# A transformer block on one core: fewer first dummy matmuls, in fp32; one filler matmul moved; the second scale sums made to wait for all their rows

## Chip, cores and metric

One core of one Trainium2 chip. The metric is the device time in microseconds; the 6 executions of the kernel before lie within 0.4% (243.81 to 244.73). A "span" is the time between the first and last instruction of the profiled execution, 1.2 to 1.5 us less than that execution's device time.

## The reference

A diffusion transformer block: six modulation vectors from `c`, layer norm with scale and shift, attention with two heads, a gated residual, a second layer norm, an MLP, a gated residual. All inputs are bf16.

```python
B, N, D = (2, 256, 1152)          # H = 2, Dh = 576, F = 4608
mod = (_silu(c) @ w_mod).reshape(B, 6, 1, D)
shift_a, scale_a, gate_a, shift_m, scale_m, gate_m = [mod[:, i] for i in range(6)]
h = _layernorm(x, axis=-1) * (1 + scale_a) + shift_a
qkv = (h @ wqkv).reshape(B, N, 3, H, Dh)
# ... attention, x = x + gate_a * a, second layer norm, MLP, gated residual (cut)
```

Only the first 20 us matter here: layer norm of x, `1 + scale_a` from `w_mod`, and the K projection.

## The kernel before

The kernel lists units of work per engine with the regions that they read and write. A scheduler derives the waits and emits each engine's instructions; TensorE keeps the written order. A semaphore is a counter on which engines wait. Every instruction other than a DMA adds 1 to its engine's semaphore (an "increment" below), and a DMA adds 16 to its own:

```python
for (k, v) in waits[ins.gidx]:
    eng_handle.wait_ge(dma_sems[k[1]] if k[0] == "d" else sems[k[1]], v)   # shortened
bi = ins.fn(eng_handle)
if ins.dma_sem is not None:
    bi.then_inc(dma_sems[ins.dma_sem], 16)
else:
    bi.then_inc(sems[e], 1)
```

The loads, in the order in which they are issued: x, the first scale weights (columns of 4 of 9 groups, in three parts of rows), K rows 0 to 3, the second scale weights (the other 5 groups, three parts), K rows 4 to 8, and so on.

```python
for (ka, kb) in ((0, KC), (KC, KT)):                      # KC = 4, KT = 9
    w = (kb - ka) * P
    for k0, k1 in ((0, 3), (3, 6), (6, 9)):
        dma(WSC[:, k0:k1, ka * P:kb * P], wmod_v[...], (k1 - k0) * P * w * 2, "ld_sc%d_%d" % (ka, k0), run=w * 2)   # shortened
    for kt in range(ka, kb):
        dma(WK[:, kt, :], wqkv_v[:, kt, D:2 * D], P * D * 2, "ld_wk%d" % kt, run=2304)
```

Dummy matmuls on zeros keep TensorE busy before there is work. The K projection runs in two parts: the first (K rows 0 to 3) while the second scale weights arrive, then 45 matmuls of 2 columns ("second scale sums"), then the second part. VectorE scales the K input between the sums and the second part; filler matmuls ("k12") in two pieces cover that.

```python
dve(270, lambda e: e.memset(Q4B, 0.0), [], [Q4B], "zq4b")
for i in range(5):
    S.unit("pe", 430.0, "warm_a%d" % i)
    mm(ps32(5), IDENT, Q4B, True, True)
CT_PS = ps16(6, 0, 18)
S.unit("pe", 100, "c_T")
tr(CT_PS, CSB[0:18, :], IDENT[0:18, 0:18])                # then tanh (ScalarE) and silu (VectorE)
# ... cut
def k12(part):
    kts = ((range(3), ()), (range(3, KC), range(KC)))[part]
    # ... 3 matmuls in the first piece, 5 in the second
for kt in range(KT):
    if kt == 6:
        k12(0)
    mod_kt(WSC, kt, 0, "scb_%d" % kt, (KC, KT))           # 5 matmuls of 2 columns
hk(KC, 0)                                                 # VectorE scales the K input
# ... cut
k12(1)
```

## Time and profile before

| | before |
|---|---|
| device time, median of 6 runs | 244.24 us (243.81 to 244.73) |
| span of the profiled execution (one of 243.62 us) | 242.3 us |
| TensorE busy | 98% of the span |
| first transposes / start of the K projection | 7.98 / 11.18 us |
| second scale sums / second K part | 17.44 / 19.63 us |

The profile is read in this order: the page's slices and its chain, the chain in order of time, then what the weight loads (PEld) waited for. The lines are in the prediction below. Starts of single matmuls, landings of DMAs and DMA packets come from the same trace's records, where each landing of x or of weights is 16 updates of a semaphore, read here as one from each of the 16 DMA engines.

### The profile page before, as it was taken

The page shows a single profiled execution, that of the slowest core. Times are in us where ns is not written, and L with a number is a line of the kernel's source. Part 1 is how long each engine was busy: PE and PEld are TensorE (multiplying, and loading weights), DVE is VectorE, ACT ScalarE, POOL GpSimd, SP SyncE. Part 2 cuts the span into 40 slices and gives each one's busy share as a digit, 9 for nine tenths or more (in the row PEclk, how much of TensorE's full clock was granted, in tenths as well). Part 3 has the DMA queues.
Part 4 walks back from the last instruction along what each step waited for, and adds up shares of the span by engine and source line. Part 5 has one row for each costly group of instructions (what it writes and reads, how often), then busy time and mean ns, then how long its engine had stood idle before and what let it go on. Part 6 is the DMA issues. An engine that isn't in the chain of part 4 may idle for free.

```text
span 242.3 us, 4076 instructions
## 1 busy us (share of the span) xinstructions
PE 238.4 (98%) x1763; PEld 147.5 (61%) x1763; DVE 120.3 (50%) x218; ACT 67.0 (28%) x136; POOL 21.2 (9%) x39
## 2 busy tenths in 40 slices
PE   7999999999999999999999999999999999999996
PEld 2698854556667666898444444444566656656676
DVE  3814388696997699789999500000022222111112
ACT  5820350355424107973233322222000000000000
POOL 1400000000021186400000000020000000000000
PEclk9999999999999999999999999999999999999999
DMA  6999999999996999989953498012000000000001
GB/s 241 330 381 392 391 392 391 397 413 405 391 356 196 351 395 391 391 266 394 314 164 82 150 320 313 0 29 72 0 16 19 16 16 19 16 16 16 19 24 27
DMA packets 30140, 51.59 MB, mean 213 GB/s; under 512 B 1703, under 2 KB 15787, under 8 KB 30123
## 3 DMA queue, kind: packets, MB, share of 16 engines
q1 hardware_dynamic: 29680, 50.14, 58.0%
q0 software_dynamic: 416, 1.19, 1.6%
q8 instruction: 14, 0.23, 0.4%
q14 instruction: 3, 0.02, 0.0%
q10 hardware_dynamic: 27, 0.00, 0.0%
HBM read 50.14 MB, written 1.19 MB: 212 GB/s over the span
## 4 chain that ended last, share of the span: by engine, by line
PE 97%; DVE 2%; POOL 0%; issue 0%; ACT 0%; DVEq 0%; POOLq 0%
PE psum L688 95%; PE psum L691 2%; DVE arena L739 1%; DVE arena L760 0%; POOL arena L711 0%; DVE arena L740 0%; DVE arena L1284 0%; DVE arena L1285 0%; POOL arena L710 0%; ACT arena L726 0%; DVE arena L727 0%; DVE arena L732 0%; DVE arena L742 0%; POOL arena L717 0%; POOL arena L715 0%
## 5 line engine op out<-in xcount | busy, mean ns | idle before, releaser
L688 PE MATMUL psum<-arena 128*128 128x384 bf16 (+10 forms) x1674 | 234.9, 306 | 1.6 <-POOL arena L711 1.5
L688 PEld LDWEIGHTS psum<-arena 128*128 128x128 bf16 (+3 forms) x1674 | 142.3, 97 | 90.0 <-issue 3.8
L1079 DVE SCALAR_TENSOR_TENSOR arena<-arena 128x1152 f32<-128x1152 bf16 x32 | 44.7, 1414 | 0.6
L1284 DVE TENSOR_TENSOR arena<-psum,arena 128x384 f32<-128x384 f32 (+3 forms) x14 | 7.0, 501 | 68.0 <-PE psum L688 68.0
L1193 ACT ACTIVATE arena<-psum 128x512 bf16<-128x512 f32 (+1 forms) x44 | 22.4, 520 | 42.7 <-PE psum L688 42.7
L683 ACT ACTIVATE arena<-psum 128x512 bf16<-128x512 f32 (+6 forms) x37 | 19.6, 549 | 39.5 <-PE psum L688 37.1
L685 DVE CAST arena<-psum 128x512 bf16<-128x512 f32 (+3 forms) x13 | 8.2, 641 | 11.4 <-PE psum L688 11.3
L669 POOL DMA_DIRECT2D dit_scratch<-arena x3 | 1.8, 616 | 115.7 <-DVE arena L685 58.9
L1161 POOL TENSOR_TENSOR arena<-arena 128x384 f32<-128x384 f32 x12 | 10.9, 910 | 10.8 <-DVE arena L1160 9.5
L1106 DVE CAST arena<-psum 72x32 bf16<-72x32 f32 x1 | 0.2, 186 | 21.3 <-PE psum L688 21.3
L739 DVE BATCH_NORM_STATS2 arena<-arena 128x6 f32<-128x384 f32 (+1 forms) x18 | 9.5, 552 | 0.1
L1166 ACT ACTIVATE arena<-arena 128x1152 bf16<-128x1152 f32 x4 | 5.3, 1345 | 11.9 <-DVE arena L1165 11.9
L691 PEld LDWEIGHTS psum<-arena 128*128 128x128 bf16 (+1 forms) x89 | 5.8, 98 | 2.5 <-issue 0.8
L1160 DVE TENSOR_TENSOR arena<-psum,arena 128x384 f32<-128x384 f32 x12 | 6.5, 549 | 1.6 <-DMA arena<-dit_scratch 1.6
L1285 DVE TENSOR_TENSOR arena<-arena 128x384 bf16<-128x384 f32 (+3 forms) x14 | 7.0, 501 | 0.5
L691 PE MATMUL psum<-arena 128*128 128x128 bf16 (+1 forms) x89 | 7.1, 219 | 0.1
L1180 DVE TENSOR_SCALAR arena<-psum,arena 128x128 bf16<-128x128 bf16 x20 | 5.4, 341 | 1.9 <-PE psum L691 1.9
L1183 ACT ACTIVATE arena<-psum,arena 128x128 bf16<-128x128 bf16 x16 | 6.0, 456 | 0.9 <-PE psum L688 0.6
L1086 DVE TENSOR_REDUCE arena<-arena 128x36 f32<-128x1152 f32 x4 | 5.4, 1348 | 0.0
L1083 DVE STREAM_TRANSPOSE arena<-arena 128x1152 f32<-128x1152 f32 x4 | 5.4, 1364 | 0.0
L1009 ACT ACTIVATE arena<-psum,arena 128x256 bf16<-128x256 f32 x8 | 3.7, 472 | 1.3 <-PE psum L688 0.9
L743 POOL TENSOR_TENSOR arena<-arena 128x1 f32<-128x1 f32 x6 | 3.6, 596 | 2.0 <-DVE arena L742 2.0
(48 smaller groups left out, 44.9 us busy)
## 6 DMA issues: line engine op xcount, KB each, us to landing
arena<-in_w_fc_dram SPq DMA_DIRECT2D x9, 1152.0 KB, 7.3
arena<-in_w_fc_dram SPq DMA_DIRECT2D x4, 2592.0 KB, 17.2
arena<-in_wqkv_dram SPq DMA_DIRECT2D x18, 288.0 KB, 10.2
arena<-in_w_mod_dram SPq DMA_DIRECT2D x3, 1728.0 KB, 20.2
arena<-in_w_mod_dram SPq DMA_DIRECT2D x3, 864.0 KB, 13.7
arena<-in_w_mod_dram SPq DMA_DIRECT2D x9, 288.0 KB, 10.5
arena<-in_wqkv_dram SPq DMA_DIRECT2D x1, 2592.0 KB, 16.6
arena<-in_wo_dram SPq DMA_DIRECT2D x1, 2592.0 KB, 24.4
```

What stands on the lines that cost most here:

```text
L683: act(c_act(n), lambda e: e.activation(out=dst, in_=src, func=ACTF.Copy), [src], [dst], name)
L685: dve(c_dve_psum16(n) if psum16 else c_dve_psum32(n), lambda e: e.tensor_copy(dst, src), [src], [dst], name)
L688: S.instr(lambda e: e.matmul(o, lhsT=l, rhs=r, start=st, stop=sp, **kw), reads=[l, r], writes=[o])
L691: S.instr(lambda e: e.transpose(o, i_, idn), reads=[i_, idn], writes=[o])
L739: dve(550, lambda e, s=s, o=o: e.bn_stats(out=o, in_=s), [s], [o], "bn_%s_%d" % (tag, ci))
L1079: dve(1270, lambda e, w=w, s=s, acc=acc: e.scalar_tensor_tensor(out=acc, in0=w, scalar=s, in1=acc, op0=ALU.mult, op1=ALU.add), [w, s, acc] ...
L1160: dve(550, lambda e, o=o, ga=ga, x1c=x1c: e.tensor_tensor(out=x1c, in0=o, in1=ga, op=ALU.mult), [o, ga], [x1c], "wo_t1_%d_%d" % (t, ci))
L1161: S.op("pool", 930, lambda e, xs=xs, x1c=x1c: e.tensor_tensor(out=x1c, in0=x1c, in1=xs, op=ALU.add), reads=[x1c, xs], writes=[x1c], name=" ...
L1183: act(440, lambda e, o=o, dst=dst, s1=s1, s2=s2: e.activation(out=dst, in_=o, func=ACTF.Identity, scale=s1, bias=s2), [o, s1, s2], [dst], ...
L1193: act(c_act(ntok), lambda e: e.activation(out=dst, in_=o, func=ACTF.Gelu_apprx_tanh), [o], [dst], "gelu_%d_%d" % (f, tok0))
L1284: dve(c_dve_psum32(w), lambda e, o=o, gm=gm, t1=t1: e.tensor_tensor(out=t1, in0=o, in1=gm, op=ALU.mult), [o, gm], [t1], "fc2_t1_%d_%d" % ( ...
L1285: dve(c_dve_32(w), lambda e, t1=t1, x1c=x1c, ost=ost: e.tensor_tensor(out=ost, in0=t1, in1=x1c, op=ALU.add), [t1, x1c], [ost], "fc2_out_%d ...
```

## The change

The intent, as far as the code tells: let the transpose of c come earlier (fewer, longer dummies in front of it, with one fp32 matmul in place of several in bf16), shorten the hole ahead of the second K part by moving a filler matmul, and let TensorE's sequencer wait once for all rows of the second scale weights.

```diff
-        dve(270, lambda e: e.memset(Q4B, 0.0), [], [Q4B], "zq4b")
-        for i in range(5):
-            S.unit("pe", 430.0, "warm_a%d" % i)
-            mm(ps32(5), IDENT, Q4B, True, True)
+        ZF = sb(O_Q4B, 2048, F32)
+        dve(400, lambda e: e.memset(ZF, 0.0), [], [ZF], "zq4b")
+        def warm32(tag, n=512, cost=1700.0, behind=None):
+            S.unit("pe", cost, "warm32_%s" % tag)
+            mm(ps32(0, 0, n), ZF[:, 0:P], ZF[:, 0:n], True, True)
+            # ... (cut) `behind`: also wait for the instruction of that name
+        warm32("a")
@@
-        warm(7, "b")
-        for n, behind in ((1, "bn_ln1_1_1"), (1, "aggr_ln1_1"), (2, "veps_ln1_1"), (2, "rstd_ln1_1")):
-            warm(n, behind, behind)
+        warm32("b")
+        warm(2, "b")
+        warm32("c", 384, 640.0, "bn_ln1_1_2")
+        warm(1, "rstd_ln1_1", "veps_ln1_1")
+        warm(1, "rstd_ln1_1", "rstd_ln1_1")
         xn_T(1)
         sca(0, 3)
         warm(1, "d")
         sca(3, 6)
-        warm(1, "f", "aggr_ln1_2")
         xn_T(0)
@@
-            kts = ((range(3), ()), (range(3, KC), range(KC)))[part]
+            kts = ((range(2), ()), (range(2, KC), range(KC)))[part]
@@
             mod_kt(WSC, kt, 0, "scb_%d" % kt, (KC, KT))
+            if kt == 0:
+                S.cur_unit.instrs[0].deps.update(j for j in S.instrs if j.name.startswith("ld_sc%d_" % KC))
```

More of the change, by code (lines that the diff above doesn't have):

```diff
@@ L717, in build_kernel @@
             S.op("pool", 100, lambda e, o=o: e.memset(ROWS[:, o:o + 64], 0.0), writes=[ROWS[:, o:o + 64]], name="rowpad%d" % o)
-        dve(270, lambda e: e.memset(Q4B, 0.0), [], [Q4B], "zq4b")
-        for i in range(5):
-            S.unit("pe", 430.0, "warm_a%d" % i)
-            mm(ps32(5), IDENT, Q4B, True, True)
+        ZF = sb(O_Q4B, 2048, F32)
[3 more added lines that the diff above has]
+            mm(ps32(0, 0, n), ZF[:, 0:P], ZF[:, 0:n], True, True)
+            if behind:
+                S.instrs[-1].deps.update(j for j in S.instrs[:-1] if j.name == behind)
+        warm32("a")
         CT_PS = ps16(6, 0, 18)
```

## The prediction

Passages that rested on knowledge from outside this case are cut out of the recorded text, and the cuts are marked. What helps to read the rest:

- "The clock opens" means that the spacing of 512-column dummies falls from 427 to 216 ns ("half rate" is the former, "full clock" the latter, where 384 columns take 162 ns). That it would open at about 5 us again is an estimate from the one trace's 4.97.
- A "pass" of an fp32 matmul stands for the time of one bf16 matmul of as many columns. In the trace before, 72 columns take 62 ns from the first record to the second, where bf16 at 216 ns for 512 would take 30; in the changed kernel's trace, the second record of a 512-column dummy takes 854 ns to the next start (4.71 to 5.56), where bf16 takes 427. The four passes are an estimate: two records of about two each.
- The "34 such" are EventSemaphore instructions.
- The second rival (the clock): 244.5 to 246 us.

> **What bounds the kernel now**
>
> I read the page's slices first, then the chain that ended last, then the weight loads' waits and the timeline of the first 20 us, where all of the edited code runs. Slices and chain:
>
> ```profile
> PE   7999999999999999999999999999999999999996
> DMA  6999999999996999989953498012000000000001
> PE 97%; DVE 2%; POOL 0%; issue 0%; ACT 0%; DVEq 0%; POOLq 0%
> ```
>
> TensorE is busy in every slice and 97% of the chain is TensorE: the kernel is a dense stream of matmuls with a head in front of it. A change helps only by starting that stream earlier or by closing a hole in it. Transfers are also busy in the first 12 slices, so early on the stream may be held by its weights. The chain in order of time tells how the head is built:
>
> ```profile
> 1.50 2.31 PE psum L688 x5
> 3.81 0.14 PE psum L691
> ...
> 3.97 0.20 ACT arena L726
> ...
> 4.27 0.19 DVE arena L727
> ...
> 4.49 0.18 DVE arena L732
> 4.66 1.40 DVE arena L739 x3
> ...
> 7.44 0.49 DVE arena L760
> ...
> 7.98 0.68 PE psum L691 x9
> ```
>
> Columns are start, length and what ran. Five dummy matmuls come first; behind them in TensorE's order the transpose of c (3.81); behind that the tanh on ScalarE and the two steps of silu on VectorE (to 4.66); and only then, because VectorE keeps its order, the layer norm statistics, which lead to the first transposes at 7.98. The chain says "dummy matmuls delay everything". But a chain names one releaser per step, so I ask the weight loads from 8.4 to 11.3 what they waited for:
>
> ```profile
> 9.11 0.41 PEld L688 LDWEIGHTS psum<-arena 128*128 128x128 bf16 x13 [0.23 <-DMA arena<-in_w_mod_dram]
> 9.45 0.70 PEld L691 LDWEIGHTS psum<-arena 128*128 128x128 bf16 x9
> 10.32 0.38 PEld L688 LDWEIGHTS psum<-arena 128*128 128x128 bf16 x12 [0.17 <-DMA arena<-in_w_mod_dram]
> ```
>
> Here the stream already waits for transfers, twice. In the trace's semaphore records the three parts of the first scale weights land at 7.99, 9.07 and 10.28 us, and the first four rows of the K weights at 11.05, 11.80, 12.55 and 13.35. The matmuls that need them start at 8.49, 9.11, 10.33, 11.18, and so on. So whatever happens before 9 us, TensorE meets the transfers again at 9.11, 10.33 and 11.18. From 11.18 to 19.5 every start follows the one before it by the length of its own stream (109 ns for 256 columns, 27 ns for 2 columns); there is no hole over 15 ns. The one hole is near the end of the second scale sums:
>
> ```profile
> 17.11 2.80 PE L688 MATMUL psum<-arena 128*128 128x256 bf16 x57
> ...
> 19.28 0.29 DVE L805 TENSOR_SCALAR arena<-arena,psum 128x256 bf16<-128x256 bf16 x1 [4.47 <-PE psum L688]
> ...
> 19.62 0.11 PEld L688 LDWEIGHTS psum<-arena 128*128 128x128 bf16 x2 [0.24 <-DVE arena L805]
> ```
>
> The last filler matmul starts at 19.398, the next at 19.630, 232 ns later instead of 109: TensorE waits 123 ns for the scaled K input that VectorE finished at 19.573.
>
> [...]
>
> [...] 512-column dummies start 427 ns apart at first and 216 ns apart later; the one that spans the change puts it at 4.97 us, 3.47 us after the first at 1.50. The page's PEclk row shows nothing of it.
>
> [...] the one 72-column fp32 matmul near 90 us stands as two records, and the second starts 62 ns after the first[...]. Two records of two passes each.
>
> [...] The old memset stands as 256 uint32 in 272 ns; no other VectorE memset here tests the slope.
>
> [...] The trace has 34 such on TensorE's sequencer, 51 ns each. The one for the first K weights starts at 11.076, 26 ns after the landing; the weight load follows at 11.152 and the matmul at 11.184, 134 ns after the landing. Waits carried by the instruction itself were quicker: 9.07 to 9.112 and 10.28 to 10.325, about 45 ns.
>
> **The change, part by part**
>
> First dummies. The memset covers 512 fp32 elements, estimated at twice 272 ns, so it ends near 1.46 instead of 1.19. The old start also waited for the identity matrix (1.44); the new one needs only the zeros, so TensorE starts near 1.51, as before. Old: 5 x 427 = 2.13 us. New: 4 passes x 427 = 1.71 us. The transpose of c moves from 3.74 to about 3.74 - 0.42 + 0.02 = 3.34; c landed at 2.21, so it is free. Tanh and silu then end near 4.26 instead of 4.66. But the statistics need x, whose first half lands at 4.33 (ScalarE's own sum starts at 4.36). So they start near 4.38 instead of 4.58: 0.2 us of the 0.4 survives.
>
> Remaining dummies. Old: 7 + 1 + 1 + 2 + 2 of 512 columns. New: one fp32 of 512 (at most 1.71 us, less after the clock opens), two bf16, one fp32 of 384 columns behind the last statistic (4 x 160 = 0.64 us at full clock), and one bf16 each behind the next two steps. They run from about 3.5 to 7.2 with holes of about half a microsecond, like the old ones, so the clock should open at about the same 5 us. All are shorter than the VectorE chain beside them, so they cost nothing, and xn follows at 7.16: the first transposes start near 7.78, 0.2 us earlier.
>
> Where these 0.2 us go. Transposes and first sums end 0.2 us earlier, then TensorE stands until 9.07 + 0.045 = 9.11 exactly as before. The wait grows, nothing else. The dummy removed ahead of the next transposes (216 ns, at 9.445) lets these start at 9.45 instead of 9.66, provided xn_0 is there (it ended at 9.34, now about 9.14); then TensorE stands until 10.28 + 0.045. Again only the wait grows, from 0.16 to 0.38 us. At 11.18 nothing is left of either gain: 0.
>
> Moved filler. Two parts had 3 and 5 matmuls; now 2 and 6. One matmul of 108 ns moves from before the last sums to after them. VectorE's input is then ready 108 ns earlier relative to the stream, and the filler is 108 ns longer: the hole of 123 ns shrinks to about 15. Saves 0.11 us. The K rows it needs landed at 19.35, so with the 134 ns of a sequencer wait the next matmul cannot start before 19.48; the new place, 19.63 - 0.11 = 19.52, is just allowed.
>
> New wait. The second scale sums began at 17.440; their rows landed at 14.69, 16.06 and 17.39. The old first sum needed only the first part; the last part was needed at 18.56, 1.2 us late. Now three waits stand on the first sum[...]: 17.39 + 0.134 = 17.52 against 17.44, a new stall of about 0.08 us.
>
> Sum: 0 (head) - 0.11 (filler) + 0.08 (wait) = -0.03 us. No instruction after 20 us changes, and the stream there has no hole that depends on a transfer.
>
> **The rivals**
>
> The head carries through. If the transfers are a little faster than in this profile, up to 0.2 us of the head and 0.2 us of the removed dummy appear: about 243.9. For it: the chain view. Against it: the two DMA waits at 9.11 and 10.32, which that chain hides.
>
> The clock opens late. [...] The transposes from 7.78 on would run at half rate, but they sit in front of DMA waits. [...] Nothing in the profile speaks for it.
>
> The sequencer wait costs more. [...] if transfers run 0.3 us late, the full delay shows at 17.4 where the old kernel had 1.2 us of slack: about 244.6. For it: the margin of 0.05 us at 17.39.
>
> **Range and chances**
>
> The old runs are 243.81, 244.30 and 244.73, and the profiled one 243.62; their mean is 244.1 and their spread exceeds every effect above. I take 244.1 (the sum of -0.03 on that mean, rounded) and 243.4 to 244.8. A 2% change would be 4.9 us; no rival reaches it. Faster 0.01, same 0.98, slower 0.01.
>
> **What would show it right or wrong**
>
> Right: first VectorE statistics near 4.4, first transposes near 7.8, but the weight loads' DMA waits grown from 0.4 to about 0.8 us in total, and the K stream still starting near 11.2; the hole at 19.6 gone; a stall up to 0.1 us at the first of the second scale sums. Wrong: the K stream starting clearly before 11.1, 512-column spacing still 427 ns after 6 us, landings of the same weights moved by more than 0.2 us, or a difference over 1 us after 20 us.

## The result

The changed kernel took 244.69 us (median of 6 runs, 244.07 to 245.71) against 244.24 before. Ratios here are the mean time of one kernel's fast runs over that of the other's of the same rounds, so not quite the ratio of the medians: 1.0021, 95% interval 0.9998 to 1.0045. That is inside the predicted range, and "the same" at 2%, but it leans to slower, and the repeat below gave 1.0019 (1.0005 to 1.0033). The change costs some 0.45 us (0.1 to 0.8 by the interval of the repeat).

The changed kernel's page, its chain by engine:

```profile
PE   7989999999999999999999999999999999999996
PE 98%; issue 1%; DVE 0%
```

The third slice has an 8 where before it had a 9, and "issue" has risen from 0% to 1%. The chain in order of time (start, length, what) says where:

```profile
1.51 2.08 PE psum L688 x2
3.58 0.12 PE psum L691
3.70 4.71 PE psum L688 x10
8.42 0.50 PE psum L691 x9
...
13.58 3.96 PE psum L688 x37
17.53 0.93 issue
18.46 15.38 PE psum L688 x197
```

The head is one TensorE piece now (the dummies reach the transposes), and there is a new piece: 0.93 us of "issue" at 17.53. "Issue" means that the profile shows nothing that TensorE waited for. The weight loads of the kernel before around that time, then those of the changed kernel, and last, from its VectorE timeline, its first statistics:

```profile
16.98 2.41 PEld L688 LDWEIGHTS psum<-arena 128*128 128x128 bf16 x57
```

```profile
16.91 0.34 PEld L688 LDWEIGHTS psum<-arena 128*128 128x128 bf16 x4
18.43 1.97 PEld L688 LDWEIGHTS psum<-arena 128*128 128x128 bf16 x53 [1.18 <-issue]
20.58 0.11 PEld L688 LDWEIGHTS psum<-arena 128*128 128x128 bf16 x2 [0.17 <-DVE arena L811]
```

```profile
4.81 1.48 DVE L745 BATCH_NORM_STATS2 arena<-arena 128x6 f32<-128x384 bf16 x3 [0.38 <-DMA arena<-in_x_dram]
```

Before, the loads run through; now there is a hole, and it ends at the second scale sums, exactly where the new wait stands. The records name what "issue" does not: the last part of the second scale weights was delivered by 15 of its 16 engines at 17.35 us and by the last at 18.37; the sequencer's wait ends at 18.40 and the first sum starts at 18.457. In the trace before the same part was complete at 17.39 and not needed until 18.56. The statistics started at 4.81, not at 4.38, because x landed at 4.78 in this execution (4.33 in the one before).

The differences between the two traces add up. From the start of the K projection to the one fp32 matmul near 90 us: 79.69 us after, 78.67 before. From there to the last matmul: 150.05 us in both, to 1 ns. The K projection itself started at 11.11 and 11.18. So the whole difference lies between 11.1 and 20.6 us. The hole ahead of the sums is 1.09 us in the records, and the one ahead of the second K part is 0.06 us shorter than before's (0.06 against 0.12): together the 1.02. The hole in this trace is larger than the mean cost of some 0.45 us, and so is that of the repeat (0.67). The executions without a trace must have smaller holes or an earlier K start; which, these runs do not show.

### The profile page after: what moved, and what is told of

Read it like the earlier page. It is cut to its first block, busy times and chain, and to the rows that moved or that the text cites. A ratio compares the mean times of both kernels' runs of the same rounds, so it can differ in the third digit from the quotient of the medians.

```text
span 243.4 us, 4050 instructions
## 1 busy us (share of the span) xinstructions
PE 238.1 (98%) x1745; PEld 147.7 (61%) x1754; DVE 120.6 (50%) x218; ACT 67.1 (28%) x136; POOL 21.8 (9%) x39
## 4 chain that ended last, share of the span: by engine, by line
PE 98%; issue 1%; DVE 0%
PE psum L688 96%; PE psum L691 2%; DVE arena L720 0%; DVE arena L1293 0%; DVE arena L1294 0%
## 5 line engine op out<-in xcount | busy, mean ns | idle before, releaser
L688 PE MATMUL psum<-arena 128*128 128x384 bf16 (+11 forms) x1656 | 234.9, 307 | 2.9 <-DVE arena L720 1.5
L685 DVE CAST arena<-psum 128x512 bf16<-128x512 f32 (+3 forms) x13 | 8.2, 642 | 11.4 <-PE psum L688 11.3
```

The lines of the kernel that those rows point to most:

```text
L685: dve(c_dve_psum16(n) if psum16 else c_dve_psum32(n), lambda e: e.tensor_copy(dst, src), [src], [dst], name)
L688: S.instr(lambda e: e.matmul(o, lhsT=l, rhs=r, start=st, stop=sp, **kw), reads=[l, r], writes=[o])
```

## The experiments

Theory W: the wait costs, because it asks early for the last engine of a transfer whose last engine is sometimes a microsecond late. Rival C: the fp32 dummies cost, since the clock opened late (dummy spacing was still the slow one at 7.8 us in the trace of the changed kernel, 5.0 before). Two more came up on the way: theory S on semaphore increments, theory F on the packet that makes an engine late.

What each trace showed, in us (hole: how much longer than its own stream TensorE took to the first second sum; "last sum to VectorE": start of the last sum to start of the scaling that waits for it, in ns):

| run | K row 0 landed | K start | packet starts | last scale part: 15th / 16th engine | hole | last sum to VectorE | K start to fp32 matmul |
|---|---|---|---|---|---|---|---|
| before | 11.05 | 11.18 | 16.96 | 17.08 / 17.39 | 0 | 344 | 78.67 |
| before again | 11.02 | 11.15 | 16.89 | 17.34 / 17.46 | 0 | 340 | 78.74 |
| changed | 10.97 | 11.11 | 15.72 | 17.35 / 18.37 | 1.09 | 389 | 79.69 |
| changed again | 10.85 | 11.33 | 15.96 | 17.24 / 18.17 | 0.67 | 393 | 79.27 |
| no wait | 11.08 | 11.22 | 16.31 | 17.20 / 17.36 | 0 | 424 | 78.63 |
| wait only | 11.49 | 11.63 | 16.07 | 17.73 / 18.54 | 0.75 | 339 | 79.41 |
| dummies only | 11.53 | 11.66 | 16.69 | 17.45 / 17.80 | 0 | 340 | 78.67 |
| filler only | 11.29 | 11.43 | 16.01 | 17.52 / 18.49 | 0 | 424 | 78.63 |
| one increment per unit | 10.92 | 11.12 | 16.00 | 17.20 / 18.47 | 0 | 204 | 78.58 |
| more instructions early | 11.62 | 11.75 | 13.33 | 17.89 / 18.36 | 0 | 340 | 78.67 |
| wait for two parts | 11.23 | 11.37 | 15.91 | 17.48 / 18.48 | 0 | 419 | 78.63 |
| fewer increments in the sums | 11.19 | 11.33 | 15.75 | 17.42 / 18.25 | 0 | 204 | 78.54 |
| no wait, fewer increments | 10.87 | 11.11 | 15.57 | 17.16 / 18.24 | 0 | 204 | 78.54 |

All kernels gave correct results.

### The changed kernel without the wait

```diff
-            if kt == 0:
-                S.cur_unit.instrs[0].deps.update(j for j in S.instrs if j.name.startswith("ld_sc%d_" % KC))
```

> The changed kernel without the new wait (dummies and filler as changed). Theory W: the changed kernel's 0.45 us come from the wait, which makes the second scale sums stand until the last of 16 DMA engines has delivered the last rows (18.37 us in its trace, where the other 15 were done at 17.35, and the matmul at 18.46). Without it the sums start near 17.3 with no hole over 0.1 us, the K stream of part two starts near 19.5 (20.58 with the wait), and the time is 244.0 to 244.3, 0 to 0.3 below the kernel before's. Rival C (the clock: in the changed kernel's trace it opened near 7.9 us instead of 5.0): the fp32 dummies cost it, so the time stays near 244.7.

Measured: 244.28 us against 244.19 before (the kernel before was run again with each set of experiments), ratio 1.0006 (0.9992 to 1.0020). The weight loads of its trace from 17 to 20 us:

```profile
16.91 2.51 PEld L688 LDWEIGHTS psum<-arena 128*128 128x128 bf16 x58
19.63 0.44 PEld L688 LDWEIGHTS psum<-arena 128*128 128x128 bf16 x5 [0.21 <-DVE arena L811]
```

The loads run through from 16.91 to 19.4; the hole is gone. The clock opened near 7.5 us in this trace, nearly as late as in the changed kernel's, and the K projection started at 11.22: for the clock as the cause there is nothing left. Two small misses: the time was expected 0 to 0.3 us below before's and came 0.1 above, within the noise; the second K part was expected near 19.5 and came at 19.63, of which more below.

### The kernel before with the wait alone

The same two lines added to the kernel before.

> The kernel before with the new wait alone. Theory W: slower than before by 0.1 us (where the last rows land near 17.4, as in the trace of before) up to 1.1 us (where they land near 18.4); a hole ahead of the second scale sums of just the landing of their last engine plus about 0.09 us. Rival C: as before, within 0.15 us.

Measured: 244.37 against 244.19, ratio 1.0012 (0.9995 to 1.0028). By time alone this would not be settled. The trace settles the mechanism:

```profile
16.99 0.78 PEld L688 LDWEIGHTS psum<-arena 128*128 128x128 bf16 x8
18.60 1.98 PEld L688 LDWEIGHTS psum<-arena 128*128 128x128 bf16 x53 [0.83 <-issue]
20.81 0.22 PEld L688 LDWEIGHTS psum<-arena 128*128 128x128 bf16 x3 [0.23 <-DVE arena L805]
```

The hole is there without any fp32 dummy. The last landing is 18.54 and the sum starts at 18.63, 0.09 us later, as in both traces of the changed kernel. Why this kernel's mean is nearer to before's than the changed kernel's is not settled; the intervals overlap, and the trace shown was of its slowest run.

### The kernel before with the new dummies alone

The first two hunks of the diff, and the dummy removed ahead of the second transposes.

> The kernel before with the new dummies alone (and the one dummy less ahead of the next transposes). Theory W: within 0.2 us of before, since the stream meets the transfers again at 9.1, 10.3 and 11.2 us; clock opening between 5 and 8 us. Rival C: 0.3 to 0.5 us slower, with the clock opening near 8 us again and the K stream starting later than 11.3.

Measured: 244.44 against 244.19, ratio 1.0006 (0.9991 to 1.0022). Here x landed early (4.29 us), the statistics started at 4.34, and so did the first transposes (TensorE's timeline):

```profile
7.74 0.45 PE L691 MATMUL psum<-arena 128*128 128x128 bf16 x5 [0.36 <-DVE arena L766]
```

7.74 against 7.98: the head gain that the prediction worked out, seen once undisturbed. The stream then stood 0.84 us until 9.62 for the second part of the first scale weights and 0.41 us until 10.86 for the third, and the K projection started at 11.66, because K row 0 landed only at 11.53. A faster head bought a longer wait. Rival C had named a K start later than 11.3 as its sign; but here the landing sets it, and two traces with bf16 dummies have such landings too (11.49 with the wait alone, 11.62 with more instructions early). The clock opened near 5.6 us.

Over all traces the clock, told by the dummies' spacing, opened between 4.6 and 7.8 us with bf16 dummies (seven traces) and between 4.9 and 7.9 us with fp32 (six). The type makes no difference that these traces could show.

### The moved filler alone

The `range(3)` to `range(2)` hunk alone.

> The kernel before with the moved filler matmul alone. The prediction says 0.1 us faster: the hole of 123 ns ahead of the second K part shrinks to about 15 ns. Both theories agree; if it is not faster, the K rows' landing (19.35 in the trace of before) is what the stream waits for there.

Measured: 244.11 against 244.19, ratio 0.9997 (0.9982 to 1.0011), no gain that timing resolves. The hole ahead of the second K part was 93 ns, not 15. It did not wait for the K rows (landed 19.25, needed at 19.84). VectorE started 424 ns after the last sum, where before it was 344. Moving the filler had made the semaphore later relative to the stream. The records of TensorE's semaphore show why: during the sums its increments come 34 ns apart without a break, while the matmuls start 27 ns apart. Before, 48 increments (45 sums, 3 fillers among them) take 47 x 34.2 = 1.61 us for a stream that starts over 1.50 us (17.44 to 18.94). With two fillers it is 46 x 34.2 = 1.57 for 1.38 us. The backlog grows from 0.11 to 0.19 us, by the 80 ns by which VectorE came later. The moved filler took 108 ns out of the stream but only its own 34 ns out of the row of increments: 34 ns is what it gains (78.67 to 78.63 in the table).

It is also worth seeing that in this trace the last scale part landed at 18.49, as late as in the changed kernel's, and cost nothing, since the matmul that needs it came at 18.70.

### One increment per unit of work on TensorE

In the kernel before, only the last matmul of each unit increments, and whoever depends on an earlier one waits for the last.

```diff
-                        eidx[e] += 1
+                        if e != "pe" or ins is u.instrs[0]:
+                            eidx[e] += 1
                         ins.eidx = eidx[e]
@@
-                    else:
+                    elif e != "pe" or ins is u.instrs[-1]:
                         bi.then_inc(sems[e], 1)
```

> The kernel before, but on TensorE only the last matmul of each unit of work increments its semaphore (others wait for that one). Theory S: in the traces the increments come 34 ns apart while the 2-column matmuls start 27 ns apart, so 48 of them leave the last increment some 0.12 us behind, and that is the hole of 93 to 123 ns ahead of the second K part; it is also why the moved filler shrank it by 30 ns and not by 108. With one increment per unit, VectorE starts 220 to 250 ns after the last sum instead of 340, the hole falls to 0 to 20 ns, and the time to 244.1 or less (0.1 below before, which timing can hardly resolve). Rival: the 340 ns are the latency of matmul and semaphore; then nothing changes.

Measured: 243.99 against 244.27, ratio 0.9986 (0.9971 to 1.0001). VectorE started 204 ns after the last sum, and the hole ahead of the second K part was gone. This is somewhat less than the 220 to 250 expected. Two new holes of 32 and 46 ns appeared near 11.7 us, where TensorE waits for ScalarE; probably ScalarE there waits for a whole unit instead of a part of it.

### More instructions ahead of everything

In the kernel before, 2 of the dummies exchanged for 32 of 2 columns, that is 60 instructions more (each matmul has a weight load: 1,763 of each in the trace before).

```diff
-        warm(7, "b")
+        warm(5, "b")
+        S.unit("pe", 860.0, "tiny")
+        for i in range(32):
+            mm(ps32(0, 0, 2), IDENT, Q4B[:, 0:2], True, True)
```

> The kernel before with 2 of the dummies exchanged for 32 of 2 columns, that is 60 more instructions on TensorE ahead of everything that counts. Theory F: the packet of 16 KB on the instruction queue (15.7 to 17.0 us in six traces, 1.1 us long) is TensorE's own next instructions, and it makes one DMA engine about 1 us late for all that follows. With 60 more instructions it comes about 3 us earlier, at 12.5 to 14 us, and the gap between the 15th and the 16th engine's landing jumps from 0.1 to 0.5 us to 0.8 us and more at an earlier transfer (the last K rows of the first part or the first two parts of the second scale weights). Rival: the packet has a fixed time or another cause and stays at 15.7 to 17.0. The time stays within 0.5 us of before: without the new wait the late landing is still in time.

Why: each trace so far had a packet of 16 KB on a queue named "instruction" between 15 and 17 us. 14 such packets stand in each execution, and TensorE has 3,561 recorded instructions in the trace before, 254 for each packet. That the packets carry TensorE's own instructions was the assumption, which this run tests. The queue lines of the changed kernel (15.6 to 16.9 us), and then of this one (13.3 to 14.5 us); columns are packets, MB, share of the 16 engines:

```profile
q8 instruction: 1, 0.02, 5.4%
```

```profile
q8 instruction: 1, 0.02, 5.5%
```

Measured: one run, 244.11, in the state "unknown" as all single runs. The packet came at 13.33, where the other traces have it at 15.57 to 16.96, so it goes with TensorE's own instructions: in all thirteen traces 252 to 294 of TensorE's records had started when it came, here 266. The second expectation was only half met: the first part of the second scale weights came 1.74 us after the last K row before it (1.34 before), but the gap between the 15th and 16th engine rose from 0.33 to 0.46 us only, not to 0.8, and it had been 0.50 at the first K row, ahead of the packet.

What the other twelve traces say: with a packet starting at 16.07 or before (eight traces) the last scale part's 16th engine lands 0.8 to 1.3 us after the 15th; with one at 16.31 or later (four traces) the gap is 0.1 to 0.4 us, and in three of those the gap rises to 0.8 to 1.2 us at the next transfer, the K row after it. The packet takes 1.1 us, about 1/16 of the engines' time for that while. That it holds one engine up is thus supported by the order in these traces, but not by the one run made to test it; that it is the only thing that does was not shown. Left open too is whether the wait itself brings the packet forward: all three traces with the full wait have it at 16.07 or before, but so have five of nine others of comparable code.

### The changed kernel once more

No edit.

> The changed kernel once more, unchanged. Theory W: 0.2 to 0.5 us slower than before again; in its trace a hole ahead of the second scale sums that ends about 0.09 us after the last engine's landing of their last rows, 0.1 us long if the instruction packet starts after 16.3 us and about 1 us if before. Clock: opening anywhere from 4.5 to 8 us, without effect on the start of the K stream.

Measured: 244.62 against 244.27, ratio 1.0019 (1.0005 to 1.0033). The hole was 0.67 us and ended 0.09 us after the landing at 18.17; the packet started at 15.96, so "about 1 us" was high by a third. The chain of this trace in a window from 15 to 22 us:

```profile
15.00 2.75 PE psum L688 x26
17.75 0.50 issue
18.26 3.83 PE psum L688 x67
```

### The kernel before once more

No edit.

> The kernel before once more, for a second trace: no hole ahead of the second scale sums wherever the last rows land (17.3 to 18.5 us), a hole near 120 ns ahead of the second K part, and 220.3 us from there to the last matmul, as in the six traces so far.

Measured: 243.58 in one run. No hole ahead of the sums, 119 ns ahead of the second K part, 220.27 us from there to the last matmul, as expected.

### Waiting for two parts only

The changed kernel, with the wait asking for two of the three parts.

```diff
-                S.cur_unit.instrs[0].deps.update(j for j in S.instrs if j.name.startswith("ld_sc%d_" % KC))
+                S.cur_unit.instrs[0].deps.update(j for j in S.instrs if j.name in ("ld_sc4_0", "ld_sc4_3"))
```

> The changed kernel, but the new wait asks only for the first two of the three parts of the second scale weights; the third is waited for where it is used, as before. Theory W (what costs is waiting early for the last part's last engine): the first two parts landed at 16.1 us or before in all nine comparable traces, so the wait costs nothing, the sums start within 30 ns after the filler ahead of them, and the time is that of the kernel without the wait: 0.0 to 0.2 us above before instead of 0.45. Rival (a wait of the sequencer costs by itself, whatever it waits for): a hole of 0.1 us or more ahead of the sums and 0.3 us or more over before.

Measured: 244.00 against 243.97, ratio 1.0002 (0.9988 to 1.0017). The third part landed at 18.48, as late as ever, and the weight loads run through:

```profile
16.95 2.63 PEld L688 LDWEIGHTS psum<-arena 128*128 128x128 bf16 x59
19.77 0.44 PEld L688 LDWEIGHTS psum<-arena 128*128 128x128 bf16 x5 [0.20 <-DVE arena L811]
```

The sequencer's wait is still there, but it was already met when it was reached (at 15.76; its part landed at 14.86) and took 51 ns. So the sequencer's wait cost nothing here by itself; what cost time in the changed kernel is the demand for the last part a microsecond before it is used.

### Fewer increments in the second sums alone, before and changed

The same edit of the increments as above, for units named `scb_` alone: 9 increments instead of 45. Once in the kernel before, once in the changed kernel without its wait.

> The kernel before, with one increment per 5 matmuls in the second scale sums alone (9 instead of 45). Theory S: VectorE starts 200 to 250 ns after the last sum instead of 340, the hole of about 120 ns ahead of the second K part is gone (under 20 ns) and nothing else moves; 0.1 us faster than before, 244.1 or less.

> The changed kernel without its wait, and with those fewer increments: new dummies, moved filler. If the hole is closed by the increments alone, the filler and the dummies add nothing: the same as the run above within 0.2 us, hole under 20 ns.

Measured: 243.88 against 243.97 before, ratio 0.9996 (0.9983 to 1.0009); and 244.10, ratio 1.0012 (0.9997 to 1.0027). In the first, TensorE's weight loads, and then VectorE's scaling, in the timeline:

```profile
16.90 3.29 PEld L689 LDWEIGHTS psum<-arena 128*128 128x128 bf16 x65
```

```profile
19.29 0.29 DVE L806 TENSOR_SCALAR arena<-arena,psum 128x256 bf16<-128x256 bf16 x1 [4.33 <-PE psum L689]
```

The hole ahead of the second K part is gone, and K start to the fp32 matmul is 78.54 us in both: 0.13 us below before, the whole hole. The moved filler then adds nothing. The medians of these two runs lie 0.22 us apart where at most 0.2 was expected. In time, 0.13 us is 0.05%, and neither run shows it: executions differ by several tenths by when the first K row lands (10.85 to 11.62 us in the table). No version was shown faster than before; the kernel with one increment per unit came nearest.

## Why the prediction was right or wrong

The measured time lies inside the predicted range, near its upper end (244.69 of 243.4 to 244.8), and the class held. The range was taken from the spread of the old runs and is far wider than the effect, so this does not speak for the mechanism. The sum failed: -0.03 us was predicted, and about +0.45 came. One of the prediction's own signs of being wrong came true as well: landings moved by more than 0.2 us (x by 0.45, the last scale part by 0.98).

- **Head: 0.** Right where K row 0 is what K waits for, which is the reason given. In ten of thirteen traces the K projection started 0.13 to 0.14 us after K row 0 landed, whatever the dummies. The other three (0.19 to 0.48) are those in which that row landed earliest, at 10.85 to 10.92: there the transposes ran up to the K start without a gap, so the head itself was last, and the first rival ("the head carries through") is alive in such executions. The size of its inner gain was right where x landed early (7.74 against the predicted 7.78). Not foreseen: x itself lands between 4.3 and 5.0 us, so in most traces the statistics wait for it, not for silu. The expected growth of the two DMA waits is not in the changed kernel's trace, since its transposes came later (8.25), not earlier; the dummies-only trace has it.
- **First dummy: 1.71 us.** Too short: its two records started 1.015 us apart and the stream took about 1.87 us. A second fp32 weight load (333 ns here; 285 to 333 ns for all six up to 7 us in this trace, 190 near 90 us) that is not wholly hidden would fit; no run isolates it. The transpose of c came at 3.51, not 3.34. Harmless. The memset, sized at twice 272 ns, took 485.
- **Moved filler: -0.11.** The mechanism was missed. The step took VectorE's start to move with the stream; it moves with the semaphore, whose increments come 34 ns apart. Measured: -0.03.
- **New wait: +0.08.** The term that was mis-sized, and it decided the sign. The step took the landing of 17.39 from the one trace. The latency after the landing was 0.09 us instead of the 0.134 used, but the landing itself was 18.17 to 18.54 in all three traces with the full wait: 0.67 to 1.09 us. The third rival said in words what came ("the full delay shows at 17.4 where the old kernel had 1.2 us of slack") and was given 0.3 us of lateness instead of 1. The 1.2 us that the prediction noted as slack were used: landings at 18.24 to 18.49 without the full wait cost nothing.
- **The clock opens late.** It did, in bf16 (up to 7.8 us) and fp32 (up to 7.9 us) alike, and cost nothing seen at the K start. The prediction's "Nothing in the profile speaks for it" leaned on one trace of something that varies by 3 us.
- **A reading.** Of the 34 EventSemaphore instructions in the trace before, 33 took 51 ns and one 266. Nothing in the sum rests on it.

## What to carry to other kernels

Slack between a landing and its use is not waste where landings jitter (here the last scale part's, from 17.36 to 18.54 us): a wait moved forward to "when everything is there" turns jitter of one DMA engine into a stall of the bound engine (here 0.67 to 1.09 us). Where small matmuls follow each other faster than the semaphore counts (here 27 against 34 ns), let only the last of a group count (here that closed a hole of 0.12 us in the traces; no time showed it), and look at the consumer's start, not at the producer's. One trace is one draw: before an estimate rests on a landing, see how it varies over several executions.
